# Sigmoid attention with a mixture-of-depths block: which pair of scores leads between the blocks of steps 4 and 5

## The chip, the core and the metric

The kernel runs on one core of a Trainium2 chip. The metric is the device time of one execution in microseconds (us); the median of the timed runs counts. Beside it stands the time of one execution under the hardware profiler, with a trace of every engine: TensorE (PE, with its weight loads shown apart as PEld), VectorE (DVE), ScalarE (ACT), GpSimd (POOL) and the DMA queues.

## The reference

Two blocks follow each other. Attention with a sigmoid in place of a softmax, over 8 sequences, 12 heads, 448 tokens and 64 dimensions a head:

```python
scores = scale * np.matmul(q, k.transpose(0, 1, 3, 2)) - np.log(S)
attn = 1.0 / (1.0 + np.exp(-scores))
return np.matmul(attn, v)
```

Then, for each sequence, a gate score per token; the 128 tokens with the highest score go through a two-layer block and are added back, the others stay as they are:

```python
top_idx = np.argpartition(-scores[b], capacity)[:capacity]
xe = x[b, top_idx]
h = np.maximum(xe @ w1, 0.0)
ye = h @ w2
out[b, top_idx] = x[b, top_idx] + g[:, None] * ye
```

All of it is in 32-bit floats.

## The kernel before

**Steps and slots.** Four heads of one sequence make a quad; a step `s` handles two quads, and there are 12 steps. A step's keys are cut into seven pieces, one for each slot `n` = 0 to 6. The order of all work on each engine is the order in which the program writes it; there is no scheduler. `stream` calls `slot(s, n)` and then `after(s, n)` for each slot. After slot 3 of a step, `after` calls `block(s)`, in which TensorE does matmuls of the two-layer block in its full 128 x 128 form; in the slots it works with 32 x 64 pieces of its array.

**Work of a slot.** The four heads of a quad lie in four groups of 32 partitions (h = 0 to 3). `score(s, n, e, pr, out)` at L387 (matmul at L397) makes the scores of the heads of pair `pr` (heads 0 and 1, or 2 and 3) for half `e` of the 64 dimensions. Its matmuls read partitions 32 h to 32 h + 31, and so use those 32 rows of the array: rows 0 to 63 for pair 0, rows 64 to 127 for pair 1. Its two calls (e = 0 and 1) add up in a score tile of two PSUM banks, `PA[pr]`; the two tiles show in the trace as `a`. `squash(s, n, pr, ...)` at L402 (L411) has ScalarE read the whole of that tile, both banks at once, and write the sigmoid to SBUF. `value(s, half, p, n)` at L416 (L429) multiplies by the values of a slot made some time before, and adds to the output banks `PO[x][pr]` (`o` in the trace; PO has four banks). Its matmuls use rows 32 r to 32 r + 31 with r = 2 half, 2 half + 1: rows 0 to 63 for half 0 and 64 to 127 for half 1. One call of `score` and one of `value` are each four matmuls, which the trace shows as two groups of four records.

**The order within a slot.** An ordinary slot is the loop at the end of `slot`. For half 0 and then half 1, with pair 1 beside half 0 and pair 0 beside half 1, it writes: the first score call of the pair, two value calls of the half, the second score call of the pair, the squash of the pair:

```python
for half in range(2):
    pr = 1 - half
    score(s, n, 0, pr, PA[pr])
    for a in entries(vs, i, half):
        value(vs, half, *a)
    score(s, n, 1, pr, PA[pr])
```

The scores of the next slot go to the same two tiles, so the next first score call of a pair waits until the squash of that pair has ended. Slots 4 and 5 of steps 4 to 10 have an order of their own (`first_slots`), and so has slot 3 of the steps after them (`last_slot`). `join` is a tiny write of ScalarE into an unused corner of the output banks.

**The block of step 4.** First `takes` has VectorE transpose the four output banks of step 3 to SBUF (L453), PO[0] first. Then `turn_rows` (L568) turns the chosen rows of sequence 0: three TensorE transposes of 128 x 128 into each of two banks (L580), a ScalarE copy out of each (L582, L583), and a sigmoid of the gate (L585). The list `places` says which banks these are. For step 4 (`s == NF + 1`, since NF = 3) they are the first bank of `PA[1]` and `PO[0][0]`. For step 5 the block has two matmul items, in `PO[0][0]` and `PO[1][0]`; L616 is the first of them.

Of the kernel before, what the change touches and what calls it, by code (L numbers as in the profile page):

```python
# [17 lines left out]
def kernel(  # L18
# [20 lines left out]
    NF = 3  # L39
# [4 lines left out]
    NU = 2 * NF + 1  # L44
# [28 lines left out]
    PA = [ps_a.tile([P, 2, 512], F32, name=f"a{n}") for n in range(2)]  # L73
    PO = [[None, None], [None, None]]
# [88 lines left out]
    def chunks(s, n, y):  # L163

        if s:
            return y, n, NU
        alone = n < 2 if y else 1 < n < 4
        if alone:
            return 1 - y, 2 * NA + n % 2, 2
        return y, n - 2 * (y or n > 3), NA  # L170

    def column(s, n, y):

        x, c, step = chunks(s, n, y)
        return c if s or step == NA else c - NA
# [114 lines left out]
    def attn_tile(pr, n):  # L290
        return attnp.tile([P, 2, S], F32, name=f"attn{pr}_{n}")
# [95 lines left out]
    def score(s, n, e, pr, out):  # L387

        for y in range(2):
            x, c, step = chunks(s, n, y)  # L390
            r = 2 * column(s, n, y)
            kt = turned[x] if s == 0 else heads["k", 2 * s + x]
            qt = heads["q", 2 * s + x].rearrange(
                "p (r e t) -> p e r t" if s else "p (e r t) -> p e r t", e=2, t=TT)
            for h in range(2 * pr, 2 * pr + 2):
                d = slice(h * TT, (h + 1) * TT)
                nc.tensor.matmul(  # L397
                    out[y * Dh:(y + 1) * Dh, h % 2, :S],
                    kt[d, e, r:r + 2].rearrange("d r t -> d (r t)"), qt[d, e],
                    start=(e == 0), stop=(e == 1))  # L400

    def squash(s, n, pr, psc):  # L402
        if s == 0 and n < 2:
            if n == 0 and pr == 1:
                attn["first"] = moe.tile([P, 7 * FH * P], F32, name="hidden")
            at = (2 * n + pr) * 2 * S
            a = attn["first"][:, at:at + 2 * S].rearrange("p (a s) -> p a s", a=2)
        else:
            a = attn_tile(pr, n)
        attn[s, pr, n] = a  # L410
        nc.scalar.activation(a, psc[:, :, :S], AF.Sigmoid, bias=bias_s, scale=QK_SCALE)  # L411
# [4 lines left out]
    def value(s, half, p, n):  # L416


        for r in (2 * half, 2 * half + 1):
            x, c, step = chunks(s, n, half)  # L420
            pr = r % 2 ^ p
            rows = slice(r * TT, (r + 1) * TT)
            at = column(s, n, half)
            if s == 0 and at < NA and r % 2 == 0:
                at = (at + AT) % NA
            at *= Dh
            i = done[s, x, pr] = done.get((s, x, pr), 0) + 1
            for j in range(2):
                nc.tensor.matmul(PO[x][pr][j * Dh:(j + 1) * Dh, :S],  # L429
                                 raw_v[s][rows, 2 * pr + j, at:at + Dh],  # L430
                                 attn[s, pr, n][rows, j, :],
                                 start=((s, x, pr, j) not in done), stop=(i == TB))
                done[s, x, pr, j] = True

    def join(x, by_vector=False):

        for t in PO[x]:
            if by_vector:
                nc.vector.memset(t[Dh:Dh + 1, S:S + 1], 0.0)
                continue  # L440
            nc.scalar.activation(t[Dh:Dh + 1, S:S + 1], bias_s[Dh:Dh + 1], AF.Copy)

    def takes(s, x):
        for pr in range(2):
            take(s, pr, x)
# [281 lines left out]
    def finish(item, args):  # L727
        (first_sums if item[0] == 1 else second_sums)(*args)
# [7 lines left out]
    def block(s):  # L736

        places = [PO[0][0], PO[0][1], PA[1][:, 0], PA[0][:, 0], PO[1][0], PO[1][1], PO[1][0]]
        if s == NF + 1:
            places = [PA[1][:, 0], PO[0][0]]  # L740
        elif s == NF + 2:
            places = [PO[0][0], PO[1][0]]
        for x in range(2):
            takes(s - 1, x)
        if (s, NF) in FETCHED and s > NF + 3:
            fetch(FETCHED[s, NF])
        stores(s, NF)
        if s == NF + 2:
            gate_part(2 * s - 2)
        elif s in FULL[::2]:  # L750
            gates(2 * s - 2)
        for item in BLOCKS[s]:
            if item[0] == "t":
                turn_rows(item[1], [places.pop(0) for _ in range(2)])
                if s in (6, 9):
                    load_v(s)
            else:
                finish(item, begin(item, places.pop(0)))
# [6 lines left out]
    def gates(i, own=True):  # L765
        gate_part(i)
        b, g = divmod(i, NG)
        if g == NG - 1:
            gate(b)
            if own:  # L770
                gate_own(b)
# [17 lines left out]
    LOW = {6: (1, 3, 4), 0: (0, 1, 2), 1: (1, 5, 6), 2: (0, 3, 4), 3: (0, 5, 6)}  # L789
    HIGH = {6: (1, 0, 1), 0: (1, 2, 3), 1: (1, 4, 5), 2: (0, 4, 5)}  # L790

    def first_slots(s, n):

        def u(e, pr):
            score(s, n, e, pr, PA[pr])

        if n == NF + 1:  # L800
            u(0, 1)
            value(s, 0, 0, 0)
            join(0)
            u(1, 1)
            u(0, 0)
            squash(s, n, 1, PA[1])
            value(s, 1, 0, 0)
            u(1, 0)
            squash(s, n, 0, PA[0])
            value(s, 1, 0, 1)  # L810
            value(s, 0, 1, 0)
            return
        u(0, 1)
        value(s, 0, 1, 1)
        value(s, 0, 1, 2)
        u(1, 1)
        squash(s, n, 1, PA[1])
        u(0, 0)
        value(s, 1, 0, 2)
        value(s, 1, 0, 3)  # L820
        u(1, 0)
        squash(s, n, 0, PA[0])

    def last_slot(s, n):


        p, one, two = LOW[n]
        value(s - 1, 1, 0, NU - 1)
        value(s - 1, 0, p, one)
        join(1)  # L830
        score(s, n, 0, 1, PA[1])
        value(s - 1, 0, p, two)
        score(s, n, 1, 1, PA[1])
        score(s, n, 0, 0, PA[0])
        squash(s, n, 1, PA[1])
        value(s - 1, 1, 1, NU - 1)
        score(s, n, 1, 0, PA[0])
        squash(s, n, 0, PA[0])

    FIRST = [[(0, (0,)), (1, (0, 1)), (1, (2, 3)), (0, (2, 3)), (0, (1, 4)), (0, (5, 6)),  # L840
              (1, (4, 5)), (1, (6,))],
# [14 lines left out]
    def slot(s, n):  # L856


        if s == 0 and n < NF + 1:
            if n == NF:  # L860
                first_outs.close()
                open_outs()
            psc = PA if n % 2 else outs
            for pr in (1, 0):
                for e in range(2):
                    score(s, n, e, pr, psc[pr])
                squash(s, n, pr, psc[pr])
            if n == NF:
                for half in range(2):
                    for a in entries(0, -1, half):  # L870
                        value(0, half, *a)
                for x in range(2):
                    join(x, by_vector=True)
            return
        vs, i = (s, n - NF - 1) if n > NF else (s - 1, n + NF)
        if vs in LATE and i < 2:
            first_slots(s, n)
            return
        if vs in LATE and n == NF:
            last_slot(s, n)  # L880
            return
        if vs and vs not in LATE and split(vs, i):
            one, two, u = rounds(vs)[i]
            for half in range(2):
                value(vs, half, one, u)
                join(half)
            for e in range(2):
                for pr in (1, 0):
                    score(s, n, e, pr, PA[pr])
            for half in (1, 0):  # L890
                value(vs, half, two, u)
            for pr in (1, 0):
                squash(s, n, pr, PA[pr])
            return
        for half in range(2):
            pr = 1 - half
            score(s, n, 0, pr, PA[pr])
            for a in entries(vs, i, half):
                value(vs, half, *a)
            score(s, n, 1, pr, PA[pr])  # L900
            if vs == 0 and half == 1 and i in (0, 2):
                join(0 if i else 1, by_vector=True)
            squash(s, n, pr, PA[pr])
            if i == 6 and s not in BLOCKS:
                takes(vs, half)
# [59 lines left out]
    def stores(s, n):  # L965

        for b in range(B - 1):
            full = FULL[b]
            for a, at in enumerate(((full, 4), (full, 6), (full + 1, 0), (full + 1, 1))):
                if (s, n) == (at if full < NS - 1 else (full, 3 + (a + 1) // 2)):  # L970
                    store(b, (a,))
# [138 lines left out]
```

## Time and profile before

| | us |
|---|---|
| timed runs | 430.63, 432.59, 432.59 (median 432.59) |
| the profiled execution | 434.43 |
| its span, first to last instruction | 432.6 |
| TensorE busy in the span | 424.7 |
| ScalarE busy | 190.3 |
| VectorE busy | 281.6 |

The granted TensorE clock was 1.0 of full speed throughout. The stretch that the change touches runs from about 103.5 us (the end of step 3's last piece) to about 127 us (the block of step 5) of the span. TensorE's share in pieces of three microseconds of it:

| stretch, us | PE busy | ACT busy | DVE busy |
|---|---|---|---|
| 103.4 to 106.0 (block of step 4; 2.6 long) | 2.28 | 2.22 | 1.88 |
| 108.4 to 111.4 | 3.00 | 1.52 | 2.93 |
| 114.4 to 117.4 | 3.00 | 2.01 | 2.86 |
| 120.4 to 123.4 | 3.00 | 2.01 | 0.60 |
| 123.4 to 126.4 | 3.00 | 1.79 | 1.96 |

Two things help in reading it. "Busy" means that at least one matmul is running: in the slots up to eight pieces of the array can run at once, so a TensorE that is busy all the time may still do half of what it could. And the end of a matmul record is modelled: a record of the slots lasts 0.534 us, while groups on the same rows follow each other every 0.376 us, so it is the distance of starts that shows the pace.

### The profile page before, as it was taken

Reading aid. Unit: us, or ns where it says so; the run is one execution under the profiler, and the core shown is the slowest. Engines: PE = TensorE matmul, PEld = TensorE weight load, DVE = VectorE, ACT = ScalarE, POOL = GpSimd, SP = SyncE. Lnnn points to the kernel's source line nnn. Section 1 sums busy time; section 2 is a strip of 40 time slices with the busy share of each in tenths; the row PEclk is TensorE's granted clock in tenths of the full one; section 3 lists DMA queues with packets and bytes.
Section 4 is the critical chain, followed back from the end, with each engine's and each line's share of the span. In section 5 each row is a group of like instructions: output and inputs, shape, how many; then the busy total and the mean of one; then the engine's idle time right before and its main releaser. Section 6 shows DMA issues by size and latency. Waiting matters only on the chain.

```text
span 432.6 us, 14250 instructions
## 1 busy us (share of the span) xinstructions
PE 424.7 (98%) x6324; PEld 254.7 (59%) x6324; DVE 281.6 (65%) x597; ACT 190.3 (44%) x249; POOL 48.0 (11%) x81
## 2 busy tenths in 40 slices
PE   8999999999999999999999999999999999999995
PEld 3455453545666478465447549546545859769952
DVE  4427557583967776976968636755666648983472
ACT  4666656666664633650660651563264330101100
POOL 3000001210210020100302020010020110101001
PEclk9999999999999999999999999999999999999999
DMA  6896747899863997988566887399935981821001
GB/s 191 245 273 178 285 89 155 207 209 251 252 180 74 244 296 186 261 269 204 182 224 184 240 204 152 103 265 277 264 109 116 236 241 36 162 57 77 23 1 73
DMA packets 114937, 78.64 MB, mean 182 GB/s; under 512 B 91420, under 2 KB 100892, under 8 KB 114876
## 3 DMA queue, kind: packets, MB, share of 16 engines
q1 hardware_dynamic: 107948, 62.47, 55.0%
q0 software_dynamic: 3296, 9.54, 7.6%
q10 hardware_dynamic: 3632, 5.74, 5.4%
q8 instruction: 49, 0.80, 0.8%
q14 instruction: 12, 0.10, 0.1%
HBM read 57.25 MB, written 20.48 MB: 180 GB/s over the span
## 4 chain that ended last, share of the span: by engine, by line
PE 93%; DMA 3%; ACT 1%; issue 1%; SPq 1%; DVE 1%; POOLq 0%; ACTq 0%
PE a L397 30%; PE o L429 28%; PE o L616 11%; PE o L680 11%; PE a L616 6%; PE a L680 5%; DMA rows_t<-in_k_dram 1%; DMA raw_k<-in_k_dram 1%; PE o L580 1%; ACT attn L411 1%; DMA out_dram<-xe,idx 1%; SPq L219 0%; PE a L580 0%; POOLq L1105 0%; SPq L120 0%
## 5 line engine op out<-in xcount | busy, mean ns | idle before, releaser
L397 PE MATMUL a<-qT,kT 32*64 32x448 f32 x2624 | 244.9, 537 | 0.9 <-DVE kT L153 0.5
L411 ACT ACTIVATE attn<-a,bias_s 128x896 f32<-128x896 f32 x162 | 161.4, 1007 | 86.1 <-PE a L397 81.7
L429 PE MATMUL o<-attn,raw_v 32*64 32x448 f32 x1952 | 176.6, 537 | 0.1
L397 PEld LDWEIGHTS a<-qT,kT 32*64 32x64 f32 x2624 | 95.6, 131 | 90.3 <-ACT attn L411 52.8
L429 PEld LDWEIGHTS o<-attn,raw_v 32*64 32x64 f32 x1952 | 69.5, 131 | 29.3 <-issue 22.5
L453 DVE STREAM_TRANSPOSE x_b<-o 128x448 f32<-128x448 f32 x48 | 28.1, 626 | 53.6 <-PE o L429 37.3
L429 PE MATMUL o<-attn,rows_t 32*64 32x448 f32 x448 | 41.9, 538 | 0.0
L632 ACT ACTIVATE hidden<-hidden 128x512 f32<-128x512 f32 x12 | 7.5, 630 | 65.8 <-DVE hidden L629 65.8
L629 DVE TENSOR_TENSOR hidden<-o,hidden 128x512 f32<-128x512 f32 x23 | 15.2, 687 | 24.2 <-PE o L616 24.0
L464 DVE TENSOR_REDUCE gate_p<-scr 128x14 f32<-128x448 f32 x48 | 29.8, 621 | 1.7
L461 DVE TENSOR_TENSOR scr<-x_b,wg_b 128x448 f32<-128x448 f32 x48 | 29.5, 615 | 1.1
L385 DVE STREAM_TRANSPOSE kT<-raw_k 128x448 f32<-128x448 f32 x42 | 24.1, 611 | 4.0 <-PE a L397 3.7
L376 DVE STREAM_TRANSPOSE qT<-qT 128x896 f32<-128x896 f32 x22 | 23.8, 1083 | 4.2 <-DMA qT<-in_q_dram 3.5
L616 PE MATMUL o<-rows_t,spare 128*128 128x128 f32 x216 | 25.6, 276 | 0.0
L616 PEld LDWEIGHTS o<-rows_t,spare 128*128 128x128 f32 x216 | 24.8, 192 | 1.4 <-DVE x_b L453 1.4
L680 PE MATMUL o<-spare,hidden 128*128 128x384 f32 x72 | 24.3, 487 | 0.0
L691 DVE SCALAR_TENSOR_TENSOR xe<-o,gate,xe 128x384 f32<-128x384 f32 x29 | 16.6, 612 | 9.7 <-PE o L680 9.6
L519 DVE SCALAR_TENSOR_TENSOR scr<-rep,who,tie 128x448 f32<-128x448 f32 (+1 forms) x28 | 18.9, 677 | 4.9 <-DMA rep<-scores 4.2
L535 POOL DMA_DIRECT2D ranks<-turned x28 | 14.5, 525 | 67.0 <-DVE turned L532 67.0
L429 PEld LDWEIGHTS o<-attn,rows_t 32*64 32x64 f32 x448 | 17.0, 131 | 5.7 <-issue 5.2
L429 PE MATMUL o<-attn,hidden 32*64 32x448 f32 x224 | 20.2, 535 | 0.0
L616 PEld LDWEIGHTS o<-rows_t,w_sb 128*128 128x128 f32 x168 | 19.3, 192 | 1.0 <-DVE x_b L453 0.7
(118 smaller groups left out, 392.7 us busy)
## 6 DMA issues: line engine op xcount, KB each, us to landing
qT<-in_q_dram SPq DMA_DIRECT2D x24, 448.0 KB
out_dram<-x_b SPq DMA_DIRECT2D x32, 336.0 KB
raw_k<-in_k_dram SPq DMA_DIRECT2D x21, 448.0 KB
spare<-sum SPq DMA_DIRECT2D x18, 384.0 KB
sum<-spare SPq DMA_DIRECT2D x8, 768.0 KB
raw_v<-in_v_dram ACTq DMA_DIRECT2D x24, 224.0 KB
w_sb<-in_moe_w_dram SPq DMA_DIRECT2D x6, 768.0 KB
rows_t<-in_v_dram SPq DMA_DIRECT2D x8, 224.0 KB
```

Source lines behind the costliest of these rows:

```text
L376: nc.vector.transpose(heads["q", i], heads["q", i])
L385: nc.vector.transpose(kt[:, e], t[:, e].rearrange("p (a n) d -> p n a d", a=2))
L397: nc.tensor.matmul(out[y * Dh:(y + 1) * Dh, h % 2, :S], kt[d, e, r:r + 2].rearrange("d r t -> d (r t)"), qt[d, e], start=(e == 0), stop=(e ...
L411: nc.scalar.activation(a, psc[:, :, :S], AF.Sigmoid, bias=bias_s, scale=QK_SCALE)
L429: nc.tensor.matmul(PO[x][pr][j * Dh:(j + 1) * Dh, :S], raw_v[s][rows, 2 * pr + j, at:at + Dh], attn[s, pr, n][rows, j, :], start=((s, x, p ...
L453: nc.vector.transpose(x_tiles[b][:, :, 2 * g + pr, :], PO[x][pr][:, :S].rearrange("p (r t) -> p r t", t=TT))
L461: nc.vector.tensor_tensor(out=tmp, in0=x_tiles[b][:, :, hp, :], in1=wg_b[:, hp:hp + 1, :].to_broadcast([P, TB, TT]), op=ALU.mult)
L464: nc.vector.tensor_reduce(out=gate_parts[b][:, :, hp], in_=tmp, axis=AX.X, op=ALU.add)
L519: nc.vector.scalar_tensor_tensor(out=junk[:n], in0=rep[:n], scalar=own, in1=tie[:n], op0=ALU.subtract, op1=ALU.is_gt, accum_out=place_s[:n ...
L616: nc.tensor.matmul(ps[:, f, :n], w((t * FH + f) * P, P), x[:, t, :n], start=(t == 0), stop=(t == KH - 1))
L680: nc.tensor.matmul(ps[:n, :DH], h[:, t, :n], w(t * DH, DH), start=(t == 0), stop=(t == FH - 1))
L691: nc.vector.scalar_tensor_tensor(out=xe[:n, cols], in0=ps[:n, :DH], scalar=st[b]["gate"][:n, 0:1], in1=xe[:n, cols], op0=ALU.mult, op1=ALU ...
```

## The change

There are two parts. In the block of step 4 the rows of sequence 0 are turned into both banks of `PA[1]`, instead of one bank of it and an output bank. And from slot 4 of step 4 to slot 3 of step 5 (seven slots) the order of the pairs is turned round: pair 0 leads and pair 1 follows. The order of the value halves stays. In slot 4 of step 4, which follows the turn, the calls also get a new order: both score calls of pair 0 and its squash come first, then values and pair 1.

`leads(s, n)` gives the pairs in the order in which they go; `at` counts slots, and the condition holds for slots 32 to 38, which are the seven named.

```diff
         if s == NF + 1:
-            places = [PA[1][:, 0], PO[0][0]]
+            places = [PA[1][:, 0], PA[1][:, 1]]
...
+    def leads(s, n):
+
+        at = s * NU + n
+        return (0, 1) if 0 < at - (NF + 1) * NU - NF <= NU else (1, 0)
+
     def first_slots(s, n):
+        a, b = leads(s, n)
...
-        if n == NF + 1:
-            u(0, 1)
+        if n == NF + 1 and a == 0:
+            u(0, a)
+            u(1, a)
+            squash(s, n, a, PA[a])
             value(s, 0, 0, 0)
             join(0)
-            u(1, 1)
-            u(0, 0)
-            squash(s, n, 1, PA[1])
+            u(0, b)
             value(s, 1, 0, 0)
-            u(1, 0)
-            squash(s, n, 0, PA[0])
+            u(1, b)
+            squash(s, n, b, PA[b])
             value(s, 1, 0, 1)
             value(s, 0, 1, 0)
             return
...
     def last_slot(s, n):
+        a, b = leads(s, n)
...
-        score(s, n, 0, 1, PA[1])
+        score(s, n, 0, a, PA[a])
         value(s - 1, 0, p, two)
-        score(s, n, 1, 1, PA[1])
-        score(s, n, 0, 0, PA[0])
-        squash(s, n, 1, PA[1])
+        score(s, n, 1, a, PA[a])
+        score(s, n, 0, b, PA[b])
+        squash(s, n, a, PA[a])
         value(s - 1, 1, 1, NU - 1)
-        score(s, n, 1, 0, PA[0])
-        squash(s, n, 0, PA[0])
+        score(s, n, 1, b, PA[b])
+        squash(s, n, b, PA[b])
...
         for half in range(2):
-            pr = 1 - half
+            pr = leads(s, n)[half]
             score(s, n, 0, pr, PA[pr])
```

Here `u(e, pr)` stands for `score(s, n, e, pr, PA[pr])`. Slot 5 of step 4 is changed in the same manner, with `a` and `b` in place of 1 and 0; slot 4 of all other steps keeps its order, written with `a` and `b` too. No matmul, activation, transfer or buffer is added or taken away; the order of instructions changes on TensorE and ScalarE only.

More of the change, by code (lines that the diff above doesn't have):

```diff
@@ L812, in first_slots @@
             return
-        u(0, 1)
+        if n == NF + 1:
+            u(0, a)
+            value(s, 0, 0, 0)
+            join(0)
+            u(1, a)
+            u(0, b)
+            squash(s, n, a, PA[a])
+            value(s, 1, 0, 0)
+            u(1, b)
+            squash(s, n, b, PA[b])
+            value(s, 1, 0, 1)
+            value(s, 0, 1, 0)
+            return
+        u(0, a)
         value(s, 0, 1, 1)
         value(s, 0, 1, 2)
-        u(1, 1)
-        squash(s, n, 1, PA[1])
-        u(0, 0)
+        u(1, a)
+        squash(s, n, a, PA[a])
+        u(0, b)
         value(s, 1, 0, 2)
         value(s, 1, 0, 3)
-        u(1, 0)
-        squash(s, n, 0, PA[0])
+        u(1, b)
+        squash(s, n, b, PA[b])
     def last_slot(s, n):
+        a, b = leads(s, n)
         p, one, two = LOW[n]
@@ L830, in last_slot @@
         join(1)
-        score(s, n, 0, 1, PA[1])
+        score(s, n, 0, a, PA[a])
         value(s - 1, 0, p, two)
-        score(s, n, 1, 1, PA[1])
-        score(s, n, 0, 0, PA[0])
-        squash(s, n, 1, PA[1])
+        score(s, n, 1, a, PA[a])
+        score(s, n, 0, b, PA[b])
+        squash(s, n, a, PA[a])
         value(s - 1, 1, 1, NU - 1)
-        score(s, n, 1, 0, PA[0])
-        squash(s, n, 0, PA[0])
+        score(s, n, 1, b, PA[b])
+        squash(s, n, b, PA[b])
     FIRST = [[(0, (0,)), (1, (0, 1)), (1, (2, 3)), (0, (2, 3)), (0, (1, 4)), (0, (5, 6)),
```

## The prediction, made before the changed kernel was run

> **What bounds the kernel now.** I read the page first (busy shares, the chain, the costliest groups), then TensorE's order of time around the block of step 4 and over one slot of step 5, and last ScalarE's and the weight loads' order of time there.
>
> ```profile
> PE 424.7 (98%) x6324; PEld 254.7 (59%) x6324; DVE 281.6 (65%) x597; ACT 190.3 (44%) x249; POOL 48.0 (11%) x81
> PE 93%; DMA 3%; ACT 1%; issue 1%; SPq 1%; DVE 1%; POOLq 0%; ACTq 0%
> L397 PE MATMUL a<-qT,kT 32*64 32x448 f32 x2624 | 244.9, 537 | 0.9 <-DVE kT L153 0.5
> L411 ACT ACTIVATE attn<-a,bias_s 128x896 f32<-128x896 f32 x162 | 161.4, 1007 | 86.1 <-PE a L397 81.7
> ```
>
> TensorE is busy 98% of the span and is 93% of the chain: time is lost or won where its array stands still, or half of it does. L397 are the scores, L429 the values, L411 the sigmoid ("squash"), 1.007 us each.
>
> TensorE around the block of step 4:
>
> ```profile
> 103.10 0.93 PE L429 MATMUL o<-attn,rows_t 32*64 32x448 f32 x8
> 103.96 0.55 PE L580 MATMUL a<-iden,xe 128*128 128x128 f32 x3
> 104.82 0.55 PE L580 MATMUL o<-iden,xe 128*128 128x128 f32 x3 [0.32 <-DVE x_b L453]
> 105.30 0.98 PE L397 MATMUL a<-qT,kT 32*64 32x448 f32 x8
> 105.95 0.70 PE L429 MATMUL o<-attn,raw_v 32*64 32x448 f32 x4
> ```
>
> The second three transposes wait for VectorE to empty their bank, and the first values (105.95) until ScalarE has copied the turned rows out of that same bank, which these values write. These are the waits that the change goes at.
>
> A slot of step 5, on TensorE:
>
> ```profile
> 115.04 0.63 PE L429 MATMUL o<-attn,raw_v 32*64 32x448 f32 x4
> 115.39 0.55 PE L397 MATMUL a<-qT,kT 32*64 32x448 f32 x4
> 115.42 0.63 PE L429 MATMUL o<-attn,raw_v 32*64 32x448 f32 x4
> 115.76 0.55 PE L397 MATMUL a<-qT,kT 32*64 32x448 f32 x4
> 115.79 0.63 PE L429 MATMUL o<-attn,raw_v 32*64 32x448 f32 x4
> 116.14 0.55 PE L397 MATMUL a<-qT,kT 32*64 32x448 f32 x4
> 116.17 0.90 PE L429 MATMUL o<-attn,raw_v 32*64 32x448 f32 x8
> ```
>
> Every 0.376 us a group of four score matmuls and a group of four value matmuls start almost together: two streams beside each other. The code says why. A matmul takes 32 rows of the array; the scores of pair 1 take rows 64 to 127 (h = 2, 3), those of pair 0 rows 0 to 63, the values of half 0 rows 0 to 63, of half 1 rows 64 to 127. One score call or one value call is two such groups. With pair 1 leading, the upper rows run S S S S V V V V (groups) in a slot while the lower run V V V V S S S S; eight groups each, 8 x 0.376 = 3.01 us.
>
> ScalarE, and the loads that wait for it (same stretch):
>
> ```profile
> 115.36 1.01 ACT L411 ACTIVATE attn<-a,bias_s 128x896 f32<-128x896 f32 x1 [0.45 <-PE a L397]
> 116.90 1.01 ACT L411 ACTIVATE attn<-a,bias_s 128x896 f32<-128x896 f32 x1 [0.54 <-PE a L397]
> 118.34 1.01 ACT L411 ACTIVATE attn<-a,bias_s 128x896 f32<-128x896 f32 x1 [0.42 <-PE a L397]
> ```
>
> ```profile
> 114.96 0.15 PEld L397 LDWEIGHTS a<-qT,kT 32*64 32x64 f32 x4 [0.44 <-ACT attn L411]
> 116.42 0.15 PEld L397 LDWEIGHTS a<-qT,kT 32*64 32x64 f32 x4 [0.39 <-ACT attn L411]
> 117.97 0.15 PEld L397 LDWEIGHTS a<-qT,kT 32*64 32x64 f32 x4 [0.44 <-ACT attn L411]
> ```
>
> Each pair has one two-bank tile of scores. Pair 1's last group starts at 116.14, its squash runs 116.90 to 117.91, and the next slot's loads come at 117.97. What covers this trip is the four value groups on the same rows; they end at 116.14 + 5 x 0.376 = 118.02. Slack: 0.05 us.
>
> **What the Trainium skill says.** "TensorE: Matmul & The Clock Gate", Part 3: work overlaps only where the row groups differ. The trace agrees: groups of one row half are never under 0.376 us apart here. The same part calls matmuls strictly first in, first out; here the trace differs: the second score call of the slot (from 115.76) starts before the last value group ahead of it in the program (116.17). So one half can be some four groups ahead of the other, and I price the new order by half, not by program order. "TensorEngine Tiling (Array Packing)", Key Properties: changing the tiling mode drains TensorE. Agreed: transposes start 0.11 us apart in a three (three in 0.55 with the tail), but the next score comes 0.2 after the last transpose's start. "PSUM — Partial Sum Buffer", on bank collisions: TensorE must not write a bank that ScalarE is reading; so the wait for the squash is not to be avoided with one tile a pair.
>
> **The change part by part.** (1) *Turn in two banks of one tile.* Same six transposes, two copies and gate; no instruction more or less. Both banks are free once pair 1's squash has ended (103.73), so six run on from 103.96 at 0.11 each and the scores of pair 0, whose own squash ended at 104.62, start near 104.76 instead of 105.30: 0.54 us won. The copies (0.49 each, second at about 105.0) now end near 105.45 instead of 105.90, and the values of half 0 wait only for VectorE's two transposes out of their banks (105.30), not for the copy.
>
> (2) *Slot 4 of step 4*, reordered: lower rows S S S S V V then V V at its end, upper rows S S V V S S V V. Pair 1's scores can start at 105.5 (copies done), its values at 106.46 (VectorE's fourth transpose ends 106.36). Then the next scores of pair 1 are due: their last group is at 107.6, and I add the trip below: 109.3. No DVE, POOL, SP or DMA instruction moves.
>
> (3) *The lead turned round, slots 5 and 6 of step 4 and 0 to 3 of step 5.* Halves of values keep their order, pairs do not. So lower rows now run S S V V V V S S, the next slot again S S ...: pair 0's scores of one slot end right where pair 0's of the next begin, with nothing of those rows between to cover the squash. The trip from the start of the last group to the next score: 0.62 until the squash starts (0.57 from the last record, 117.77, to 118.34; 0.67 from the group's first), 1.01 squash, 0.05 to the load, 0.05 to the matmul = 1.73 us, against 0.376 when groups follow each other. Loss 1.35 a slot, on the lower rows and, one after the other, on the upper rows too. A slot takes 7 x 0.376 + 1.73 = 4.36 us. Queued behind the waiting load on TensorE are the values and the other pair's scores; ScalarE and VectorE wait for these in turn, but have spare time (ScalarE 2.0 of 3.0 us a slot).
>
> Sum, along the upper rows, which end last: slot 5 starts at 109.3; + 4.36 x 4 = 126.75 for slot 2 of step 5, whose last score group is at 129.4; last slot (two value groups come first, but the trip is longer): scores at 129.4 + 1.73 = 131.1, then six groups (S S V V S S), end 131.1 + 6 x 0.376 = 133.4. Before, by the same reckoning 56 groups a half from 105.95 end at 127.0, and the trace shows the last group at 126.7 and the block of step 5 at 127.25. So +6.3 us, the 0.54 already in it. From step 5's block on everything is as before, and TensorE is the chain there, so nothing gives it back; VectorE gets slack that I cost at nothing, as it was not what the block of step 5 waited for longest (0.7 us, which might go).
>
> Bounds: 0.5 to 0.74 until the squash starts gives +5.8 to +7.0. How far one half may run ahead the trace shows only from below; at three groups instead of four or more it is about +7.7.
>
> The profiled execution took 434.43 us with a span of 432.6; the three timed runs 430.63 to 432.59, median 432.59. Span 438.9, and on the median 438.9.
>
> **Rivals.**
> A, forecast: the bare trip, +6.3: 438.9.
> B: look-ahead is short, as strict order would make it. With two groups, the lower rows' eight must mostly be through before the upper rows start: a slot takes 12 groups = 4.5 us plus, +10.7: 443. Against it: 115.76 before 116.17 above.
> C, not slower: the trip stays covered. It decides at the turn of each slot on one half of the rows: if the next score follows its forerunner within 0.376 + 0.05 us, not 1.73, each half needs 56 groups; upper rows from 105.55, 0.16 lost in slot 4: 105.55 + 21.06 + 0.16 = 126.8, 0.3 less than before: 432.3. For it: the wait is already there in every slot (weight loads wait 0.4 for ScalarE) and costs TensorE nothing. Against: that is so by four value groups on the same rows, and they are what moves away.
> D: the change does what it says and VectorE's or the queue's later waits shrink by some of the 6 us: 437. The chain's 1% each for ACT and DVE leave it little.
>
> **How the numbers follow.** A 0.78, B 0.05, C 0.08, D 0.09. What a measurement can tell from no change is about 0.5%, 2.2 us. C's gain is below that; 0.05 of it counts as same, 0.03 as faster, should timing scatter (the runs above spread by 2 us). A, B and D are slower: 0.92. Range: A's +5.8 to +7.7, D's lower end, and 1 us of scatter: 436.2 to 441.0.
>
> **What would show it.** Right: six transposes without a gap from 103.96 and scores by 104.8; then slots of about 4.4 us instead of 3.0 from 109 to 127, with holes in the stream of each half, ScalarE's squash just before each; PE still "busy" by the page, because one half runs on; the block of step 5 near 133.6. Wrong: score groups of the same pair 0.38 us apart across a slot's turn (C), or the two halves no longer beside each other (B).

## The result, and the profile after

| | before | after |
|---|---|---|
| median of four timed runs each, us | 432.19 | 438.38 (438.07 to 438.61) |
| span of the profiled execution | 432.6 | 436.3 |
| first transpose of step 4's block | 103.96 | 103.50 |
| first matmul of step 5's block (L616) | 127.25 | 134.10 |
| from the one to the other ("the stretch") | 23.3 | 30.6 |
| from there to the end of the span | 305.4 | 302.2 |

The changed kernel takes 1.0159 times as long, 95% interval 1.014 to 1.0178 (the quotient of the two medians alone, 1.0143, lies at the lower end of it). The stretch grew by 7.3 us; the rest of the profiled execution is 3.2 us shorter, which needs an explanation of its own. A hint: the profiled execution of the kernel before took 434.43 us, more than any of its four timed runs (430.63 to 432.59). The page of the changed kernel (busy time of each engine, the chain by engine, two of the costliest groups):

```profile
PE 429.1 (98%) x6324; PEld 255.3 (59%) x6324; DVE 281.5 (65%) x597; ACT 190.4 (44%) x249; POOL 47.9 (11%) x81
PE 94%; DMA 3%; issue 1%; DVE 1%; SPq 1%; POOLq 0%; ACT 0%; ACTq 0%
L397 PE MATMUL a<-qT,kT 32*64 32x448 f32 x2624 | 243.1, 538 | 0.6 <-DVE kT L153 0.5
L411 ACT ACTIVATE attn<-a,bias_s 128x896 f32<-128x896 f32 x162 | 161.6, 1007 | 90.8 <-PE a L397 88.0
```

Of the slowdown this page shows almost nothing: TensorE is busy 98% as before, since one half of its rows works on while the other waits. Only ScalarE's idle time before its squashes grew, from 86.1 to 90.8 us. TensorE's order of time around step 4's block shows more:

```profile
103.50 0.88 PE L580 MATMUL a<-iden,xe 128*128 128x128 f32 x6
104.31 2.01 PE L397 MATMUL a<-qT,kT 32*64 32x448 f32 x24
...
105.86 1.21 PE L429 MATMUL o<-attn,raw_v 32*64 32x448 f32 x16
...
107.51 1.07 PE L429 MATMUL o<-attn,raw_v 32*64 32x448 f32 x16
108.31 0.93 PE L397 MATMUL a<-qT,kT 32*64 32x448 f32 x8
```

The turn is now one row of six transposes; the scores come 0.81 us after its start, where they came 1.34 after it. Next ScalarE's order of time, from slot 4 of step 4 on and over two slots of step 5 (L441 is the corner write, `join`):

```profile
106.17 1.01 ACT L411 ACTIVATE attn<-a,bias_s 128x896 f32<-128x896 f32 x1 [0.79 <-PE a L397]
107.20 0.26 ACT L441 ACTIVATE o<-bias_s 1x1 f32<-1x1 f32 x2
107.89 1.01 ACT L411 ACTIVATE attn<-a,bias_s 128x896 f32<-128x896 f32 x1 [0.44 <-PE a L397]
...
115.93 1.01 ACT L411 ACTIVATE attn<-a,bias_s 128x896 f32<-128x896 f32 x1 [1.77 <-PE a L397]
117.54 1.01 ACT L411 ACTIVATE attn<-a,bias_s 128x896 f32<-128x896 f32 x1 [0.60 <-PE a L397]
120.29 1.01 ACT L411 ACTIVATE attn<-a,bias_s 128x896 f32<-128x896 f32 x1 [1.74 <-PE a L397]
```

Pair 0's squash comes at 115.93 and again at 120.29: 4.36 us a slot, where before it was 3.0. In front of it ScalarE idles for 1.7 us: the squash waits for scores and the scores for the squash before. The weight loads show the other side of this:

```profile
114.93 0.15 PEld L397 LDWEIGHTS a<-qT,kT 32*64 32x64 f32 x4
...
116.52 0.15 PEld L397 LDWEIGHTS a<-qT,kT 32*64 32x64 f32 x4 [0.22 <-issue]
116.99 0.20 PEld L397 LDWEIGHTS a<-qT,kT 32*64 32x64 f32 x8 [0.32 <-ACT attn L411]
```

At 114.93 the weights of pair 0's last group are loaded; its matmuls follow 0.38 later, when the group ahead of it is through. Its squash ends at 116.94, and 0.05 later, at 116.99, pair 0's next slot is loaded. The load at 116.52 is pair 1's. So no new group starts on the lower rows from 115.31 to 116.99: they stand idle for the trip.

### The profile page after: what moved, and what is told of

It is laid out like the page before. It is cut to its first block, busy times and chain, and to the rows that moved or that the text cites. A ratio compares the mean times of both kernels' runs of the same rounds, so it can differ in the third digit from the quotient of the medians.

```text
span 436.3 us, 14251 instructions
## 1 busy us (share of the span) xinstructions
PE 429.1 (98%) x6324; PEld 255.3 (59%) x6324; DVE 281.5 (65%) x597; ACT 190.4 (44%) x249; POOL 47.9 (11%) x81
## 4 chain that ended last, share of the span: by engine, by line
PE 94%; DMA 3%; issue 1%; DVE 1%; SPq 1%; POOLq 0%; ACT 0%; ACTq 0%
PE a L397 30%; PE o L429 29%; PE o L616 11%; PE o L680 11%; PE a L616 6%; PE a L680 5%; DMA raw_k<-in_k_dram 1%; PE o L580 1%; DMA qT<-in_q_dram 1%; DMA out_dram<-xe,idx 1%; PE a L580 0%; SPq L219 0%; POOLq L1124 0%; DVE qT L381 0%; ACT attn L411 0%
## 5 line engine op out<-in xcount | busy, mean ns | idle before, releaser
L411 ACT ACTIVATE attn<-a,bias_s 128x896 f32<-128x896 f32 x162 | 161.6, 1007 | 90.8 <-PE a L397 88.0
L397 PEld LDWEIGHTS a<-qT,kT 32*64 32x64 f32 x2624 | 93.9, 131 | 88.4 <-ACT attn L411 50.3
L429 PEld LDWEIGHTS o<-attn,raw_v 32*64 32x64 f32 x1952 | 68.6, 131 | 34.4 <-issue 27.6
L616 PE MATMUL o<-rows_t,spare 128*128 128x128 f32 x216 | 25.6, 276 | 0.0
L616 PEld LDWEIGHTS o<-rows_t,spare 128*128 128x128 f32 x216 | 24.7, 192 | 1.4 <-DVE x_b L453 1.4
L616 PEld LDWEIGHTS o<-rows_t,w_sb 128*128 128x128 f32 x168 | 19.3, 192 | 1.0 <-DVE x_b L453 0.7
```

Source lines behind the costliest of these rows:

```text
L397: nc.tensor.matmul(out[y * Dh:(y + 1) * Dh, h % 2, :S], kt[d, e, r:r + 2].rearrange("d r t -> d (r t)"), qt[d, e], start=(e == 0), stop=(e ...
L429: nc.tensor.matmul(PO[x][pr][j * Dh:(j + 1) * Dh, :S], raw_v[s][rows, 2 * pr + j, at:at + Dh], attn[s, pr, n][rows, j, :], start=((s, x, p ...
L616: nc.tensor.matmul(ps[:, f, :n], w((t * FH + f) * P, P), x[:, t, :n], start=(t == 0), stop=(t == KH - 1))
```

## The experiments

All share the reading from the first transpose of step 4's block to the first matmul of step 5's block; where only one run was made, its time is that run's. Diffs are against the changed kernel unless the text says otherwise; "..." stands for lines left out.

**The turned order without the turn's new places (lead_only).**

```diff
-            places = [PA[1][:, 0], PA[1][:, 1]]
+            places = [PA[1][:, 0], PO[0][0]]
```

> Only the lead is turned round; the rows of sequence 0 are turned into one bank of pair 1's tile and an output bank, as in the kernel before. Measured on the stretch from the first transpose of step 4's block to the first matmul of step 5's block (23.29 us before, 30.60 after). Theory (a pair's scores follow each other on the same rows, so the trip through ScalarE lies open): about 30.9, as the turn in two banks is worth only some 0.3 to 0.5. Rival (the new places of the turn make the loss): about 23.3.

The stretch was 31.1 us, the time 439.45 (before beside it: 430.73). The loss is in the order; the new places won 0.5 us of it back.

**The turn's new places without the turned order (turn_only).** This is the kernel before with this edit:

```diff
-            places = [PA[1][:, 0], PO[0][0]]
+            places = [PA[1][:, 0], PA[1][:, 1]]
```

> Kernel before, with only the turn moved to both banks of pair 1's tile; pair 1 still leads. The scores of pair 1 then wait for both copies out of that tile, but the first values of half 0 no longer wait for the second copy. Theory: stretch from the first transpose to step 5's block about 23.0 us (before 23.29); the time is the same within what scatters elsewhere. Rival (the two banks as such cost time): clearly over 23.3.

The stretch was 23.3 us, as before, where 0.3 less had been expected; the time 431.77, the ratio to the kernel before 0.9987 (0.9969 to 1.0005). TensorE's order of time in it:

```profile
103.62 0.88 PE L580 MATMUL a<-iden,xe 128*128 128x128 f32 x6
105.46 0.60 PE L397 MATMUL a<-qT,kT 32*64 32x448 f32 x4 [0.96 <-ACT rows_t L583]
105.59 0.72 PE L429 MATMUL o<-attn,raw_v 32*64 32x448 f32 x4
```

The transposes no longer pause, but the pair that leads here writes the very banks that hold the turned rows, and waits for the second copy out of them. The 0.5 us pause has only moved. The new places pay only where the other pair leads behind the turn.

**Squash before values (cover).** In slots 5 and 6 of step 4 and 0 to 2 of step 5, both score calls of a pair and its squash come ahead of the values of that half, in the same form for slot 5 (`early` is true where pair 0 leads):

```diff
             score(s, n, 0, pr, PA[pr])
+            if early:
+                score(s, n, 1, pr, PA[pr])
+                squash(s, n, pr, PA[pr])
             for a in entries(vs, i, half):
                 value(vs, half, *a)
+            if early:
+                continue
             score(s, n, 1, pr, PA[pr])
...
```

Five corner writes (`join`) were added, which keep the order of values that share a bank.

> Pair 0 still leads, but in the ordinary slots of the range and slot 5 of step 4 both score calls of a pair come first, then its squash, and then the two value calls on the same rows. Five small joins keep value calls on different rows of one output bank apart. The program still has eight groups of one row half in a row. Theory (the trip lies open): four value groups, 1.5 us, stand between the scores of a pair and the next ones, so a slot is near 3.0 us again and the stretch about 24.9 with a look-ahead of four groups. Rival (TensorE follows the program's order and one half idles while the other's eight groups run; the trip is beside the point): still 4.4 us a slot, stretch 30 or more.

The stretch was 26.2 us, the time 433.22 (before beside it: 430.73). ScalarE's squashes in it, the first and third being pair 0's in two successive slots, and TensorE's loads:

```profile
109.89 1.01 ACT L411 ACTIVATE attn<-a,bias_s 128x896 f32<-128x896 f32 x1 [1.16 <-PE a L397]
111.53 1.01 ACT L411 ACTIVATE attn<-a,bias_s 128x896 f32<-128x896 f32 x1 [0.63 <-PE a L397]
113.19 1.01 ACT L411 ACTIVATE attn<-a,bias_s 128x896 f32<-128x896 f32 x1 [0.66 <-PE a L397]
```

```profile
112.57 0.18 PEld L429 LDWEIGHTS o<-attn,raw_v 32*64 32x64 f32 x4 [0.20 <-issue]
112.95 0.18 PEld L429 LDWEIGHTS o<-attn,raw_v 32*64 32x64 f32 x4 [0.20 <-issue]
113.00 0.21 PEld L397 LDWEIGHTS a<-qT,kT 32*64 32x64 f32 x8
```

A slot takes 3.3 us, with the same pair in the lead: what moved is that the four value groups now stand behind the squash of their rows (and five corner writes came in), and the trip is covered again. The loss of 1.36 a slot was the bare trip. The 1.3 us missed against the expectation are about what the 0.3 a slot that stay come to. The loads show where these come from: pair 1's load (113.00) comes just after the fifth lower group since pair 0's scores has started, although no squash holds it up: pair 1's had ended at 112.54. (A group's weights are loaded when the group ahead of it starts: the load at 112.57 is the fifth group's, and at 112.95 that group starts and the sixth is loaded.) With eight lower groups in one block, the upper rows start late in every slot.

**The values turned round with the pairs (mirror).** The halves of the values change places too, in slot 5 of step 4 to slot 2 of step 5:

```diff
-        for half in range(2):
-            pr = leads(s, n)[half]
+        for half in reversed(leads(s, n)):
+            pr = 1 - half
...
```

Slot 5 of step 4 has the same order, written out, and slot 3 of step 5 keeps the order of before.

> Changed kernel with the value halves turned round together with the pairs from slot 5 of step 4 to slot 2 of step 5 (half 1 beside pair 0, half 0 beside pair 1); slot 3 of step 5 in the order of before. The lead is turned round, the two row halves work beside each other again. Theory: 3.0 us a slot, stretch about 23.6 us, time as before within 0.5%. Rival (a turned lead costs by itself, by buffers or the changed order on ScalarE): 4.4 us a slot, near 30.

The stretch was 23.7 us, the time 432.27, the ratio to the kernel before 1.0011 (0.9995 to 1.0028). TensorE's order of time inside a slot, and at the slot where pair 1 leads again:

```profile
116.22 0.55 PE L429 MATMUL o<-attn,raw_v 32*64 32x448 f32 x4
116.30 0.55 PE L397 MATMUL a<-qT,kT 32*64 32x448 f32 x4
116.59 0.55 PE L429 MATMUL o<-attn,raw_v 32*64 32x448 f32 x4
116.67 0.55 PE L397 MATMUL a<-qT,kT 32*64 32x448 f32 x4
...
124.74 0.60 PE L397 MATMUL a<-qT,kT 32*64 32x448 f32 x4 [0.38 <-ACT attn L411]
```

Groups on the same rows are 0.37 us apart again, scores of one half beside values of the other. Pair 0 leads as in the changed kernel, at the old pace. So it isn't the pair that costs, but that the scores of a pair end and begin on the same rows with nothing between. Where the lead goes back to pair 1 there is one stop: no matmul starts for 0.91 us ahead of 124.74.

**The lead turned in one slot (one_slot).** Pair 0 leads in slot 4 of step 4 alone:

```diff
-        return (0, 1) if 0 < at - (NF + 1) * NU - NF <= NU else (1, 0)
+        return (0, 1) if at == (NF + 1) * NU + NF + 1 else (1, 0)
```

> Changed kernel with pair 0 leading in slot 4 of step 4 only, the slot that follows the turn; from slot 5 on the order of before. Theory: only one place is left where pair 1's scores follow each other with too little between, and the rows can catch up; stretch about 23.6 us, time as before within 0.5%. Rival (the loss is made in slot 4 by the join and the new order there): stretch 25 or more.

The stretch was 24.4 us, the time 432.17, the ratio to the kernel before 1.0018 (1.0 to 1.0036). It lies between what was expected and the rival. TensorE's order of time where the lead goes back to pair 1:

```profile
107.17 1.07 PE L429 MATMUL o<-attn,raw_v 32*64 32x448 f32 x16
108.62 0.60 PE L397 MATMUL a<-qT,kT 32*64 32x448 f32 x4 [0.38 <-ACT attn L411]
```

Pair 1's scores of slot 5 wait for its own squash, which has only just run (107.56 to 108.57), and the values stand behind them in the program; no matmul starts for 0.91 us. The win of the turn is more than spent there: the stretch is 1.1 us longer than before, though the time shows no difference.

**A shorter squash (half_squash).** In the seven slots ScalarE makes the sigmoid of the first head of a pair alone; that of the second head is left out, and GpSimd sets it to zero:

```diff
+        if s and leads(s, n)[0] == 0:
+            nc.gpsimd.memset(a[:, 1], 0.0)
+            nc.scalar.activation(a[:, 0], psc[:, 0, :S], AF.Sigmoid, bias=bias_s, scale=QK_SCALE)
+            return
```

> Changed kernel; in the seven slots the squash is done for the first head of each pair only, the second head's part is set to zero by GpSimd: the sigmoid of half the heads is left out in these slots. ScalarE's trip gets shorter by about 0.47 us. Theory (trip): a slot loses 0.47 us less, 3.9 instead of 4.36, stretch about 27.9. Rival (order and look-ahead): no change, 30.6.

As a whole it missed: the stretch was 35.8 us and the time 443.27. GpSimd's order of time shows why, and ScalarE's what the pace was afterwards:

```profile
112.98 2.03 POOL L539 DMA_DIRECT2D ranks<-turned  x4 [16.42 <-DVE turned L536]
...
117.82 2.55 POOL L412 MEMSET attn<- 128x448 f32 x6
```

```profile
122.10 0.63 ACT L413 ACTIVATE attn<-a,bias_s 128x448 f32<-128x448 f32 x1 [8.71 <-PE o L433]
...
126.09 0.63 ACT L413 ACTIVATE attn<-a,bias_s 128x448 f32<-128x448 f32 x1 [1.37 <-PE a L397]
```

The zeroing stood behind a DMA issue of GpSimd that waited 16.4 us for VectorE, and the values waited for the zeroing. Once that was over, pair 0's squashes came 3.99 us apart (122.10, 126.09, and so on for three slots): with a squash of 0.63 us, not 1.01, a slot was 0.37 shorter than 4.36. Here the squash's length goes into the pace one for one.

**A longer squash (longer_squash).** In the seven slots the sigmoid of a pair's first head is made twice:

```diff
+        if s and leads(s, n)[0] == 0:
+            nc.scalar.activation(a[:, 0], psc[:, 0, :S], AF.Sigmoid, bias=bias_s, scale=QK_SCALE)
```

> Changed kernel; in the seven slots ScalarE makes the sigmoid of the first head of each pair twice, once alone and once with the whole pair, so that its work on each score tile gets about 0.53 us longer (a sigmoid of one head took 0.63 us, some 0.1 of which overlaps the next). TensorE's order is untouched. Theory (trip): a slot takes 4.36 + 0.53 = 4.9 us, the stretch about 33.8 us (30.60 in the changed kernel). Rival (order and look-ahead): ScalarE has 2 us of spare time a slot, so nothing changes, 30.6.

The stretch was 34.6 us, the time 442.15. ScalarE's order of time, pair 0's squashes of two slots:

```profile
117.59 0.63 ACT L412 ACTIVATE attn<-a,bias_s 128x448 f32<-128x448 f32 x1 [1.77 <-PE a L397]
118.26 1.01 ACT L413 ACTIVATE attn<-a,bias_s 128x896 f32<-128x896 f32 x1
...
122.62 0.64 ACT L412 ACTIVATE attn<-a,bias_s 128x448 f32<-128x448 f32 x1 [1.74 <-PE a L397]
```

A slot takes 5.03 us, 0.67 more than in the changed kernel, where 0.53 had been expected; 0.67 is the distance of starts of the two squashes (117.59 to 118.26). ScalarE idles for 1.7 us before the first of them: it isn't short of time, and yet each piece of its work lengthens the slot. Both runs say that the trip is a loop of TensorE and ScalarE in which neither may start before the other has ended.

**Upper scores two groups earlier (early_upper).** In slots 5 and 6 of step 4 and 0 to 2 of step 5, pair 1's first score call stands ahead of pair 0's second one (slot 5 in the same way):

```diff
+        turned = leads(s, n) == (0, 1)
         for half in range(2):
             pr = leads(s, n)[half]
-            score(s, n, 0, pr, PA[pr])
+            if not (turned and half):
+                score(s, n, 0, pr, PA[pr])
             for a in entries(vs, i, half):
                 value(vs, half, *a)
+            if turned and not half:
+                score(s, n, 0, 1, PA[1])
             score(s, n, 1, pr, PA[pr])
...
```

> The changed kernel, with pair 1's first score call written ahead of pair 0's second one, not behind it, in slots 5 and 6 of step 4 and 0 to 2 of step 5; all else as there. What it asks: what holds the upper rows back, so that the stretch from the first transpose of step 4's block to the first matmul of step 5's block came out at 30.6 us where 29.3 + 0.3 was reckoned. If it is that one row half can be only four groups ahead of the other in the program (pair 1's load comes with the start of the fifth lower group, 109.84), two groups less stand before it here, pair 1's scores of slot 5 start as soon as its squash is through (some 5.6 us after the first transpose, not 6.3), and the stretch is about 0.65 shorter, 29.95 us, at the same 4.36 us a slot. If the upper rows are held back by something else (their own squash, the copies, the corner writes), the stretch stays at 30.6.

The stretch was 30.0 us. Its loads, then those of the changed kernel, where pair 1's scores of slot 5 come, and the changed kernel's matmuls there:

```profile
109.50 0.15 PEld L429 LDWEIGHTS o<-attn,raw_v 32*64 32x64 f32 x4 [0.22 <-issue]
109.52 0.21 PEld L397 LDWEIGHTS a<-qT,kT 32*64 32x64 f32 x8
```

```profile
109.44 0.15 PEld L429 LDWEIGHTS o<-attn,raw_v 32*64 32x64 f32 x4 [0.22 <-issue]
109.82 0.15 PEld L429 LDWEIGHTS o<-attn,raw_v 32*64 32x64 f32 x4 [0.22 <-issue]
109.84 0.21 PEld L397 LDWEIGHTS a<-qT,kT 32*64 32x64 f32 x8
```

```profile
108.31 0.93 PE L397 MATMUL a<-qT,kT 32*64 32x448 f32 x8
109.06 1.31 PE L429 MATMUL o<-attn,raw_v 32*64 32x448 f32 x12
109.85 0.61 PE L397 MATMUL a<-qT,kT 32*64 32x448 f32 x4
```

Counted from each kernel's first transpose (103.94 here), pair 1's scores are loaded after 5.58 us, not 6.34, and the stretch is 0.6 us shorter at the same pace of a slot. So the upper rows were held back by the groups ahead of them in the program. In the changed kernel pair 1's squash had ended at 108.90; its load came only when the fifth lower group since pair 0's scores started (two groups from 108.31 on, three from 109.06 on, the last of these at 109.81). Eight lower groups stand ahead there, so three were still to start. In early_upper six stand ahead, and the load came when the third started (109.50): again three were still to start, although pair 1's squash had ended at 109.34.

Two timed runs took 440.26 and 440.55 us, beside 432.7 to 437.9 for the kernel before: ratio 1.0124, interval 0.9978 to 1.0269, too wide to rank it against the changed kernel. Its trace is of use for something else, too (next section).

**The changed kernel again (after_again)**, to see whether the 3.2 us given back later are a gain of the change:

> The changed kernel again, in more runs, next to more runs of the kernel before. The stretch is 7.3 us longer, but the medians are only 6.2 us apart, and the profiled execution of before loses 3.2 us in six short stops after the stretch that the changed kernel's doesn't have. If such stops come by chance in any kernel, more runs of the changed kernel scatter as before's do (430.1 to 434.6) and the difference of medians is near 7.3. If the change keeps them away, its runs stay within 438.0 to 438.7 and the difference stays near 6.4.

The median of six runs was 438.64 us (438.12 to 439.24), of ten of the kernel before 432.2 (430.2 to 433.74): ratio 1.0158 (1.0131 to 1.0184). The difference stays at 6.4 us, and the kernel before scatters by 3.5 us where this one scatters by 1.1.

## The 3.2 us behind the stretch

In the profiled execution of the kernel before, TensorE makes short stops behind the stretch that the changed kernel's doesn't make. At the first of them, before, ScalarE's squashes and the weight load that ends the stop:

```profile
175.66 1.99 ACT L411 ACTIVATE attn<-a,bias_s 128x896 f32<-128x896 f32 x2 [1.22 <-PE a L397]
176.72 0.15 PEld L397 LDWEIGHTS a<-qT,kT 32*64 32x64 f32 x4 [0.90 <-ACT attn L411]
```

and in the profile of early_upper, at the same place of the program:

```profile
182.76 1.99 ACT L411 ACTIVATE attn<-a,bias_s 128x896 f32<-128x896 f32 x2 [1.06 <-PE a L397]
183.82 0.15 PEld L397 LDWEIGHTS a<-qT,kT 32*64 32x64 f32 x4 [0.90 <-ACT attn L411]
```

In both no matmul starts for about 0.65 us there, and so it is, for 0.56 to 0.65 us, at three more places (at 207.2, 289.6 and 311.7 us before; 214.3, 295.7 and 317.8 in early_upper). The kernel before has one more, of 0.58 us, at 250.9, which no squash ends. At the four places that both have, ScalarE runs the squashes of both pairs one behind the other, and the load that ends the stop comes 0.05 us after the first of the two has ended. At the first place the changed kernel's squashes start one by one, 1.5 us apart. So the stop is the trip over a score tile again, bare in that slot.

From step 5's block to the end the kernel before takes 305.4 us and early_upper 304.8, the changed kernel (both profiles) and the seven other experiments between 301.9 and 302.5. So an execution with pair 0 in the lead can have these stops, and turn_only, mirror and one_slot, which run at the pace of the kernel before, can be without them: it looks as if the 3.2 us come and go with the execution, and aren't a gain of the change. The kernel before was traced only once, but the spans of its untraced runs, 428.3 to 432.8 us, fit: its traced 432.6 without the 3.2 would be 429.4. Why the trip is covered at these places in one execution and bare in another stays open. Open, too, is why the changed kernel's ten timed runs scatter less, and so why the medians differ by 6.2 to 6.4 and not by the stretch's 7.3: the kernel before seems to lose about 1 us to such stops in the middle of its runs, but timed runs have no trace.

## Why the prediction was right

*The turn (1).* 0.54 us were forecast, 0.53 came: 0.81 us from the first transpose to the scores, not 1.34. turn_only adds what the prediction didn't say: with pair 1 in the lead the places alone win nothing.

*The pace (3).* 4.36 us a slot were forecast, from 7 x 0.376 plus a trip of 1.73. Measured: 4.36. (In the trace the matmul follows its load at once, so the trip is 1.68, and the group behind it comes after 0.43, not 0.376; the sum is the same.) cover and mirror take the exposed trip away and the pace with it; half_squash and longer_squash change the squash by -0.38 and +0.67, and the pace by -0.37 and +0.67. Rival C (the trip stays covered) falls by these, and rival B (hardly any look-ahead, 10.7 us) by the 7.3.

*Slot 4 and the start of slot 5 (2): mis-sized by 1.0 us.* Pair 1's scores of slot 5 were put at 109.3, 5.34 us after the first transpose. They came 6.34 after it, and every later slot is as late; so the stretch grew by 7.3, not 6.3. The step reckoned with the squash of pair 1 alone, and that one was nearly on time: it ended 5.40 after the first transpose. The other 0.9 the scores waited for groups of the lower rows that stand ahead of them in the program. early_upper shows it: with two of these fewer, they were loaded 0.76 earlier, and the stretch was 0.6 shorter. The prediction had "some four groups" of look-ahead and kept three for the upper bound (7.7), but its sum took the look-ahead to cost nothing; counted by groups that are still to start, it was three, the case that the bound stood for (7.7; 7.3 came).

Part of the wait is that the lower rows themselves were late, and here the corner write fits: in ScalarE's lines above it stands behind pair 0's squash (106.17 to 107.18), ends at 107.46, and 0.05 later, at 107.51, the values start that are kept in order by it; the lower rows had been free since about 106.6. By a reckoning in groups, with three upper ones still to start, they could have gone on at 106.9, so this delays pair 0's scores of slot 5, and pair 1's with them, by about 0.6. That is an estimate; no run took the corner write alone. Both effects lie in one chain, so their shares can't be added up to the 1.0.

*What the sum lacked (D).* 438.9 against a median of 438.38 is closer than its parts, and that is luck: misses of opposite sign. For the span it is 2.6 us too much (436.3): 1.0 too little in step (2), against 3.2 behind step 5's block and 0.5 ahead of step 4's, where the prediction let nothing differ and executions do. It started from the span of an execution that had the stops. Rival D had a shorter rest in mind too, but from later waits that shrink because of the slowdown. turn_only speaks against it: it isn't slower, and its rest is as short (302.1). VectorE's wait there, which "might go", is 0.7 us as before, although VectorE had slack: it idles for 8.9 us ahead of that block, until the last values in its banks are through, and these are as late as everything else.

*Program order.* The Trainium skill ("TensorE: Matmul & The Clock Gate", Part 3) has matmuls strictly first in, first out. The traces differ: a half does run ahead of program order (115.76 before 116.17 in the kernel before), but where it was counted (last section) not while more than three groups ahead of it in the program were still to start. For a count by halves both facts are needed.

## What to carry to other kernels

Here a round trip TensorE, ScalarE, TensorE over one tile was free only while other work on the same rows of the array stood between its two ends. So before an order is turned round, write out what runs on each half of the rows, and look at what follows a tile's last scores. The busy share, 98% before and after, didn't show the loss: read the distance of starts on the same rows, and ScalarE's idle time before the squash. Where two orders belong together, as pairs and value halves here, turn both or neither, and look at the slots in which the lead changes.

## What the runs showed of the hardware

- How far one half of the rows runs ahead of the other: in three traces a group started only when no more than three groups of the other half that stand ahead of it in the program were still to start. In the changed kernel and in cover eight stand ahead, and the load comes as the fifth starts (109.81 and 109.84; 112.95 and 113.00); in early_upper six stand ahead, and it comes as the third starts (109.50 and 109.52). In all three the squash of the tile had ended 0.2 to 0.9 us before.
- The trip over a score tile of two banks, bare: 0.62 us from the last group's start to the squash, 1.01 for the squash, 0.05 to the next load, whose matmul starts within 0.01: 1.68.
- TensorE's short stops, 0.56 to 0.66 us without a new matmul each, at the same four places of the program in two executions (granted clock 1.0 in both) and absent in nine others. Each of the eight ends 0.05 us after the end of a squash.
